# The last nine head pairs of an attention and MLP kernel: q and k loaded by tokens and transposed by DMA

## The chip, the cores and the metric

The kernel runs on one core of one Trainium2 chip. The metric is the device time of one execution in microseconds. A core has TensorE (PE, matrix products into the eight banks of PSUM), ScalarE (ACT), VectorE (DVE), GpSimd (POOL), the queue engine SyncE (SP) and 16 DMA engines. Every engine works through its own list of instructions in order and waits on semaphores. DMAs can be issued from SP, ACT and POOL; a DMA that changes the type from float32 to bfloat16 on the way is issued from POOL in this kernel.

## The reference

```
q, k, v: 8 x 8 heads x 576 tokens x 64, float32
q_d, k_d, v_d = means over groups of 4 tokens           (144 coarse tokens)
out_d     = softmax(q_d k_d^T / 8) v_d, each row repeated 4 times
out_local = softmax over |i - j| < 4 of (q k^T / 8), times v
x   = (out_up + out_local) as 4608 tokens x 512
h   = x @ w_in          (512 x 2048)
out = (h * sigmoid(h)) @ w_out      (2048 x 512), float32
```

The attention is small in arithmetic and rich in instructions; the two products of the MLP are most of the arithmetic.

## The kernel before

The 64 heads are worked in 32 pairs (two heads side by side on 128 partitions). A pair passes through these steps; the letters are the names of the planner's jobs.

- `cq`, `ck`: q and k of the pair are loaded and cast to bfloat16 by one DMA each from POOL (line 676), by rows of 576 numbers: a row holds nine tokens of one head, and the tile qkb has 128 rows (k is loaded with an offset of 64 rows, so a tile holds halves of two pairs). qkb has six buffers.
- `T`: 36 transposes of 64x64 on TensorE (`pe_T`, line 810) turn q and k into [head dimension, token] in two PSUM banks.
- `eq`, `ek`: two copies from PSUM to qT and kT, on ACT from pair 8 on (line 565), which also put the tokens in order.
- `mq`, `mk`: two reductions on DVE (line 845), which sum groups of four tokens.
- `S`: 28 score products on TensorE; then two exps on ACT (line 893) and a product with the band mask on DVE (line 899).
- `Z`: sums of the softmax on TensorE, a small transpose, a reciprocal and a spread on DVE (lines 964, 968, 974).
- `PV`: 28 products with v; then the scaled result xo on DVE (line 990), and the sum of the coarse and the local part into the tile xT on POOL (line 1018).
- v is loaded from SP in two layouts (vs, in runs of 64 numbers, and vq), cast on POOL, and its groups of four are summed on POOL (lines 565, 785, 790).

From pair 8 on the attention's products on TensorE are issued in visits: visit n holds S of pair n, T of pair n+1, PV of pair n−2 and Z of pair n−1. Between the visits TensorE works on the MLP. A G1 block is four products of 512 columns that make one 128-wide slice of h for 512 tokens. ACT takes a tanh of it (line 1043), DVE multiplies (line 1047), which frees the bank, and the result is a slice of gT. A G2 block is four products of 512 columns, a quarter of an output tile of 128 tokens; after four of them ACT copies the tile out (line 1100) and SP stores it. There are 144 blocks of each kind. G1 needs xT of all pairs whose tokens it reads.

The order of all instructions is fixed when the program is built. A planner (`Plan.run`) plays the jobs through with a cost for each, releases buffers and banks, and on each engine starts the ready job with the earliest due time. On TensorE a visit is preferred over MLP blocks from a given number of finished blocks on, and G1 is preferred until it leads G2 by 22 blocks (LEAD). For a DMA a job has a cost (the issue on its engine) and a work (its time on the shared DMA engines), with fixed times before and behind it. Each engine's list is then issued in the order that the plan gave, with the waits that the data need:

```
            op.waits = [...]                      # Prog.op: what the data need
            can = [j for j in ready[e] if self.fits(j)]
            j = pick(now, can) if e == "PE" else min(can, key=lambda j: (j.due, j.idx))
```

So a change of one step can change the order of everything behind it on every engine.

Of the kernel before, what the change touches and what calls it, by code (L numbers as in the profile page):

```python
# [7 lines left out]
ALU = mybir.AluOpType  # L8
# [16 lines left out]
N_QK, N_VS, N_VQ, N_QKB, N_VB, N_VD, N_T, N_P, N_ZR, N_RB, N_XO = 1, 4, 2, 6, 5, 5, 3, 4, 2, 2, 3  # L25
GS_PE = 0
VP_PE = 8

# [466 lines left out]
def bass_hourglass_attn__then__act_silu_kernel(  # L495
# [9 lines left out]
    with kctx:  # L505
# [23 lines left out]

        qk = sb("qk", [128, 2, 576], F32, N_QK)  # L530
        vs = sb("vs", [128, 10, 64], F32, N_VS)
        vq = sb("vq", [128, 4, 256], F32, N_VQ)
# [4 lines left out]
        qT = sb("qT", [128, S_], BF16, N_T)  # L537
        kT = sb("kT", [128, S_ + 16], BF16, N_T)
        qd = sb("qd", [128, SD], BF16, N_T)
# [7 lines left out]
        for name, n, first in (("qk", N_QK, 0), ("vs", N_VS, 0), ("vq", N_VQ, VP_PE), ("vt", 1, VP_PE),  # L547
                               ("qkb", N_QKB, -1), ("vb", N_VB, 0), ("vd", N_VD, 0), ("T", N_T, 0), ("P", N_P, 0),
                               ("zr", N_ZR, 0), ("Rb", N_RB, 0), ("xo", N_XO, 0), ("th", 2, 0), ("osb", 3, 0)):
            L.pool(name, n, first, SW if name == "qk" else ())  # L550

# [61 lines left out]
        def constants():  # L613
# [44 lines left out]
            fill("pads", [(t[:, a:b], 0.0, [], [R(f"{n}{i}")]) for i in range(N_T)  # L658
                          for t, n, a, b in ((kT[i], "kTa", 0, 3), (kT[i], "kTb", 579, 592), (kd[i], "kdp", 144, 192))], -75)
            fill("hot", [(hot[:, i, :], 0.0, [], [R(f"hot{i}")]) for i in range(3)]  # L660
# [19 lines left out]
        def loads(p, order):  # L680
            if p == 0:
                dma("lkx", LD_ENG("kx", 0), lambda: kx[64:128, :], lambda: rows(k, 0, 64, 0), None, lambda: rkx, lambda: "kx",
                    0.45, 0.43, due=order["kx"], take=[("qkb", -1)])
            for x, (t, n, off) in enumerate(((q, 128, 0), (k, 128 if p < NPAIR - 1 else 64, 64))):
# [62 lines left out]
        def casts(p):  # L747
# [28 lines left out]
            def emitv(jb):  # L776
                a, b = S("vs", p), S("vb", p)
                P.op(jb.ran, lambda e: copy(jb.ran, e, vb[b][:, :, :], vs[a][:, :, :]),
                     [R(f"vs{a}{h}{j}") for h in range(2) for j in range(2)] + ([R("vz")] if p == 0 else []), [R(f"vb{b}")])
            J(f"cv{p}", CV_ENG if p < 4 else "POOL", {"POOL": 0.72, "ACT": 0.74}, emitv, pre=[f"lv{p}{h}{j}" for h in range(2) for j in range(2)],  # L780
              port=True, due=D(p, 4.8 if p < 4 else 6.0), take=[("vb", p)], use=[("vs", p)])
# [20 lines left out]
        def pe_T(p):  # L802
            a, b = S("qkb", p), S("qkb", p - 1)
            tiles = ((0, 0, 0, a), (0, 1, 1, a), (1, 1, 0, a), (1, 0, 1, b))
            for r in range(9):
                for j, h, x, n in tiles:
                    t, c = t_home(p, x, r)
                    o = PS[half(h), t, c:c + 32].bitcast(BF16)
                    w = qkb[n][half(j), x, 64 * r:64 * r + 64]
                    P.op("PE", lambda e, o=o, w=w, j=j: e.transpose(o, w, idn[half(j), :]),  # L810
                         [R("idn"), R(f"qkb{n}{x}")], [rB[t]])

        def pe_G(p):
            s, b = S("T", p), bank(("g", p))[0]
            for x, t in enumerate((qT[s][:, :], kT[s][:, 3:579])):
                for r in range(4):
                    mm(PS[:, b, 144 * x:144 * x + 144], idw[:, :], t.rearrange("p (g r) -> p r g", r=4)[:, r, :],
                       [R("idw"), R(f"{'qk'[x]}T{s}")], [rB[b]], r == 0, r == 3)

        def after_T(p):  # L820
# [3 lines left out]
            def evict(x):  # L824
                def emit(jb):
                    s = S("T", p)
                    dst = (qT[s][:, :] if x == 0 else kT[s][:, 3:579]).rearrange("p (g r) -> p g r", r=9)
# [12 lines left out]

            def reduce(x):
                def emit(jb):
                    s = S("T", p)
                    dst, src = (qd[s][:, :], qT[s][:, :]) if x == 0 else (kd[s][:, 0:SD], kT[s][:, 3:579])
                    P.op("DVE", lambda e: e.tensor_reduce(dst, src.rearrange("p (g r) -> p g r", r=4), AX.X, ALU.add),  # L845
                         [R(f"{'qk'[x]}T{s}")], [R(f"{'qk'[x]}d{s}")])
                return emit

            if grp:
                J(f"G{p}", "PE", 1.08, lambda jb: pe_G(p), pre=[f"eq{p}", f"ek{p}", "idw1"], bank=[(("g", p), G_BANKS(p))],  # L850
                  due=D(p, 7.7), use=[("T", p)], kind="A", mm=8)
            for x in range(2):
# [3 lines left out]
                if grp:  # L856
                    J(f"m{n}{p}", G_ENG(p, x), {"ACT": 0.31, "DVE": 0.27}, group(x), pre=[f"G{p}"], bank=[(("g", p), ())],
                      due=D(p, 7.4), use=[("T", p)])
                else:
                    J(f"m{n}{p}", "DVE", 0.74, reduce(x), pre=[f"e{n}{p}"], due=D(p, 7.3), **keys)  # L860

        def pe_S(p):
# [9 lines left out]
            for i in range(5):  # L872
                for h in range(2):
                    for y in range(2):
                        c, n = 58 * i, 58 if i < 4 else 56
                        t = 288 * y + c
                        mm(PS[half(y), bb[h], c:c + n], kT[s][half(h), t:t + 64], qT[s][half(h), t:t + n], rl,
                           [rB[bb[h]]], not bias, True)
# [230 lines left out]
        def tk(p):  # L1109
            return dict(use=[("qkb", p), ("qkb", p - 1)], pre=[f"cq{p}", f"ck{p}", "idn"] + (["ckx"] if p == 0 else [f"ck{p - 1}"])  # L1110
                        , bank=[(("q", p), T_BANKS(p)), (("k", p), T_BANKS(p))])
# [39 lines left out]
        def visit(n):  # L1151
            s, t = n < NPAIR, n + 1 < NPAIR
            z = n - 1 if SPLIT <= n - 1 < NPAIR else None
# [61 lines left out]
        for p in range(SPLIT + 1):  # L1215
            split(p)
        for n in range(SPLIT, NPAIR + LAG):
            visit(n)
# [78 lines left out]
```

## Time and profile before

| | us |
|---|---|
| median of three runs | 340.75 (340.31 to 341.02) |
| the profiled execution, whole | 342.31 |
| its span (first to last instruction) | 340.5 |
| TensorE busy | 326.8 |
| VectorE busy | 229.6 |
| ScalarE busy | 179.0 |
| GpSimd busy | 156.6 |
| one copy to qT or kT on ScalarE, mean | 0.66 |
| one reduction to qd or kd on VectorE, mean | 0.72 |
| issue of one load of q or k on GpSimd | 0.55 |

Busy time says which engine has work, not which one is waited for. TensorE's instructions overlap: one 64x64 transpose is shown with 201 ns, and a whole block of 36 takes about 0.3 us. What a part is worth on TensorE is therefore read from the distance between the starts of what stands before and behind it. "PEld" is the load of the stationary operand, which runs ahead of its product.

### The profile page before, as it was taken

The page shows a single profiled execution, that of the slowest core. Times are in us where ns is not written, and L with a number is a line of the kernel's source. Part 1 is how long each engine was busy: PE and PEld are TensorE (multiplying, and loading weights), DVE is VectorE, ACT ScalarE, POOL GpSimd, SP SyncE. Part 2 cuts the span into 40 slices and gives each one's busy share as a digit, 9 for nine tenths or more (in the row PEclk, how much of TensorE's full clock was granted, in tenths as well). Part 3 has the DMA queues.
Part 4 walks back from the last instruction along what each step waited for, and adds up shares of the span by engine and source line. Part 5 has one row for each costly group of instructions (what it writes and reads, how often), then busy time and mean ns, then how long its engine had stood idle before and what let it go on. Part 6 is the DMA issues. An engine that isn't in the chain of part 4 may idle for free.

```text
span 340.5 us, 10780 instructions
## 1 busy us (share of the span) xinstructions
PE 326.8 (96%) x4623; PEld 213.9 (63%) x4623; DVE 229.6 (67%) x410; ACT 179.0 (53%) x317; POOL 156.6 (46%) x211
## 2 busy tenths in 40 slices
PE   5587999999999999999999999999999999999996
PEld 2465677865555775587557755785577558866544
DVE  6586989866667885788577857796767556754200
ACT  5542756665544765476447645664656416644221
POOL 7363498435679667970698068704400140000000
PEclk9755999999999999999999999999999999999999
DMA  8997879999878976996398339500100010000112
GB/s 168 175 252 156 255 181 212 198 229 234 172 178 195 213 177 151 209 202 174 76 240 180 81 57 249 115 1 33 66 31 2 33 64 31 2 1 31 62 64 92
DMA packets 70666, 44.59 MB, mean 131 GB/s; under 512 B 45914, under 2 KB 63770, under 8 KB 70618
## 3 DMA queue, kind: packets, MB, share of 16 engines
q1 hardware_dynamic: 56378, 28.00, 30.8%
q0 software_dynamic: 13088, 15.36, 26.2%
q8 instruction: 36, 0.59, 0.7%
q10 hardware_dynamic: 1152, 0.54, 0.7%
q14 instruction: 12, 0.10, 0.1%
HBM read 45.61 MB, written 9.44 MB: 162 GB/s over the span
## 4 chain that ended last, share of the span: by engine, by line
PE 92%; DMA 2%; DVE 2%; issue 2%; POOL 1%; ACT 0%; POOLq 0%
PE PS L571 89%; PE PS L810 3%; DMA qkb<-in_k_dram 2%; DVE Pt L899 1%; POOL qkb L676 0%; DVE qd L845 0%; POOL gT L601 0%; DVE Rb L974 0%; DVE qT L565 0%; DVE kd L845 0%; DVE zt L964 0%; DVE zr L968 0%; ACT osb L1076 0%; DVE vd L565 0%; POOL idw L610 0%
## 5 line engine op out<-in xcount | busy, mean ns | idle before, releaser
L571 PE MATMUL PS<-xT,w_in_sb 128*128 128x512 f32 x576 | 141.2, 399 | 0.0
L571 PE MATMUL PS<-w_out_bf,gT 128*128 128x512 bf16 (+1 forms) x592 | 131.3, 374 | 0.0
L571 PEld LDWEIGHTS PS<-xT,w_in_sb 128*128 128x128 f32 x576 | 106.7, 188 | 24.7 <-DVE gT L1047 0.7
L1047 DVE SCALAR_TENSOR_TENSOR gT<-th,PS 128x512 bf16<-128x512 f32 x144 | 96.9, 683 | 37.0 <-ACT th L1043 36.3
L1043 ACT ACTIVATE th<-PS 128x512 f32<-128x512 f32 x144 | 86.1, 599 | 54.2 <-PE PS L571 46.0
L571 PEld LDWEIGHTS PS<-w_out_bf,gT 128*128 128x128 bf16 x592 | 54.7, 98 | 62.9 <-issue 3.5
L1018 POOL TENSOR_TENSOR xT<-xo 128x576 fp32r<-128x576 f32 (+5 forms) x48 | 43.5, 919 | 51.5 <-DVE xo L990 51.4
L565 POOL CAST vb<-vs 128x640 bf16<-128x640 f32 x32 | 24.4, 767 | 57.3 <-PE PS L571 42.5
L1100 ACT ACTIVATE osb<-PS 128x512 f32<-128x512 f32 x35 | 21.1, 603 | 53.6 <-PE PS L571 53.6
L893 ACT ACTIVATE Pt<-PS 128x576 bf16<-128x576 f32 x32 | 20.8, 649 | 33.0 <-PE PS L571 32.8
L785 POOL TENSOR_TENSOR vt<-vq 128x512 f32<-128x512 f32 x24 | 30.8, 1285 | 10.0 <-DMA vq<-in_v_dram 9.9
L990 DVE TENSOR_TENSOR xo<-PS,Rb 128x720 f32<-128x720 f32 x32 | 28.6, 893 | 5.1 <-PE PS L571 4.9
L974 DVE STREAM_TRANSPOSE Rb<-zr 128x768 f32<-128x768 f32 x32 | 30.9, 964 | 0.1
L899 DVE TENSOR_TENSOR Pt<-Pt,mask 128x576 bf16<-128x576 bf16 x24 | 16.3, 677 | 20.9 <-ACT Pt L893 20.9
L565 ACT ACTIVATE qT<-PS 128x576 bf16<-128x576 bf16 x30 | 19.8, 659 | 9.4 <-PE PS L810 9.4
L810 PE MATMUL PS<-idn,qkb 64*64 64x64 bf16 x1152 | 17.5, 201 | 7.5 <-issue 3.9
L845 DVE TENSOR_REDUCE qd<-qT 128x144 bf16<-128x576 bf16 x32 | 22.9, 716 | 1.5 <-ACT qT L565 1.4
L845 DVE TENSOR_REDUCE kd<-kT 128x144 bf16<-128x576 bf16 x32 | 23.0, 718 | 0.0
L964 DVE STREAM_TRANSPOSE zt<-PS 128x96 f32<-128x96 f32 x32 | 8.8, 274 | 20.2 <-PE PS L571 20.2
L565 ACT ACTIVATE kT<-PS 128x576 bf16<-128x576 bf16 x30 | 20.0, 665 | 1.6 <-PE PS L810 1.6
L810 PEld LDWEIGHTS PS<-idn,qkb 64*64 64x64 bf16 x1152 | 14.2, 115 | 9.5 <-issue 4.5
L676 POOL DMA_DIRECT2D qkb<-in_k_dram x31 | 17.1, 553 | 5.1 <-PE PS L810 5.1
(56 smaller groups left out, 229.3 us busy)
## 6 DMA issues: line engine op xcount, KB each, us to landing
vs<-in_v_dram SPq DMA_DIRECT2D x123, 80.0 KB, 4.6
out_dram<-osb SPq DMA_DIRECT2D x35, 256.0 KB, 3.6
vq<-in_v_dram SPq DMA_DIRECT2D x24, 256.0 KB, 4.3
qkb<-in_q_dram POOLq DMA_DIRECT2D x31, 144.0 KB, 5.0
qkb<-in_k_dram POOLq DMA_DIRECT2D x30, 144.0 KB, 5.4
w_in_sb<-in_moe_w_in_dram POOLq DMA_DIRECT2D x4, 1024.0 KB, 7.4
w_out_bf<-in_moe_w_out_dram POOLq DMA_DIRECT2D x4, 512.0 KB, 14.3
vq<-in_v_dram SPq DMA_DIRECT2D x48, 32.0 KB, 3.9
```

What stands on the lines that cost most here:

```text
L565: return e.activation(out_, in_, AF.Copy) if eng == "ACT" else e.tensor_copy(out_, in_)
L571: P.op("PE", lambda t: t.matmul(out_, lhsT, rhs, start=start, stop=stop, skip_group_check=True), r, w)
L785: P.op("POOL", lambda g: g.tensor_tensor(vt[:, :, :], vq[n][:, :, 0:128], vq[n][:, :, 128:256], ALU.add), [R(f"vqm{n}"), R(f"vqe{n}0"), R( ...
L810: P.op("PE", lambda e, o=o, w=w, j=j: e.transpose(o, w, idn[half(j), :]), [R("idn"), R(f"qkb{n}{x}")], [rB[t]])
L845: P.op("DVE", lambda e: e.tensor_reduce(dst, src.rearrange("p (g r) -> p g r", r=4), AX.X, ALU.add), [R(f"{'qk'[x]}T{s}")], [R(f"{'qk'[x]} ...
L893: P.op("ACT", lambda e: e.activation(d[:, :, :], PS[:, b[0]:b[1] + 1, a:e_], AF.Exp, scale=sc), [rB[b[0]], rB[b[1]]], [R(f"P{m}" if local ...
L974: P.op("DVE", lambda e: e.transpose(Rb[n][:, :].rearrange("p (c q) -> p c q", q=32), zr[z][:, :].unsqueeze(2).to_broadcast([128, 24, 32])) ...
L990: P.op("DVE", lambda e: e.tensor_tensor(xo[x][:, :, :], PS[:, bb[0]:bb[1] + 1, 0:360], Rb[u][:, :].rearrange("p (x c) -> p x c", x=2)[:, : ...
L1018: P.op("POOL", lambda g, dst=dst, in0=in0, in1=in1: g.tensor_tensor(dst, in0, in1, ALU.add), [R(f"xo{x}")], xblk(kc, t + a, t + e_))
L1043: P.op("ACT", lambda e: e.activation(th[x][:, :], PS[:, b, :], AF.Tanh, scale=0.5), [rB[b]], [R(f"th{x}")])
L1047: P.op("DVE", lambda e: e.scalar_tensor_tensor(gT[j % 2][:, f, :], th[x][:, :], 1.0, PS[:, b, :], ALU.add, ALU.mult), [rB[b], R(f"th{x}")] ...
L1100: P.op("ACT", lambda e, s=S("osb", n), b=bank(key)[0]: e.activation(osb[s][:, :], PS[:, b, :], AF.Copy, scale=0.5), [rB[bank(key)[0]]], [R ...
```

## The change

From pair 23 to pair 31 (`DTS`), q and k no longer go through qkb, TensorE and PSUM. Each of them is loaded by two DMAs from POOL (one for each head) into one of four tiles tq: 96 partitions, six blocks, and in each block the 64 numbers of a token of both heads. A run of 64 numbers is 256 bytes in DRAM and 128 bytes as bfloat16. Then one DMA issued from ACT transposes the six blocks of 96x128 into qT or kT. The reductions, the scores and all behind them are as before. kT's data begin at column 16 instead of 3. Three of the four tq tiles lie in the memory of qk, which only pair 0 uses. A load of pair p+2 waits until the transpose of pair p has read the tile. The casts of v may go to ACT or POOL for these pairs; in the order that the planner makes, they stay on POOL.

On TensorE nine blocks of 36 transposes fall away; on ACT 18 copies are replaced by 18 issues of a transpose; on POOL 18 loads are replaced by 36 smaller-grained ones. The due times, costs and thresholds of all other jobs are unchanged. The planner makes a new order from pair 22's visit on.

```
+DTS = tuple(range(23, NPAIR))
+KB = 16
+C_WORK, X_WORK, X_COST = 1.35, 0.95, 1.22
+X_ENG = "ACT"
...
+        tq3 = qk[0][:, :, :].rearrange("p a b -> p (a b)").bitcast(BF16)
+        tq1 = sb("tq", [128, 768], BF16)
+        tq = [tq3[:, 768 * i:768 * i + 768] for i in range(3)] + [tq1[:, :]]
...
+                if p in DTS:
+                    def emitc(jb, x=x, t=t):
+                        u = S("tq", 2 * DTS.index(p) + x)
+                        d = tq[u][0:96, :].rearrange("p (a h d) -> p a h d", a=6, h=2)
+                        for h in range(2):
+                            P.op("POOL", lambda e, h=h: e.dma_start(d[:, :, h, :], bass.AP(
+                                tensor=t.tensor, offset=t.offset + (2 * p + h) * S_ * D_, ap=[[64, 96], [96 * 64, 6], [1, 64]])),
+                                [], [R(f"tq{u}")], f"tq{u}", after=gates(["cq0", "ck0"] + list(order.get(("gate", p), ()))))
+                    J(f"c{'qk'[x]}{p}", "POOL", 1.46, emitc, work=C_WORK, gran=0.018, take=[("tq", 2 * DTS.index(p) + x)], due=D(p, 26.0),
+                      pre=["cq0", "ck0", f"c{chr(113 - 6 * x)}{p - 1}!"] + list(order.get(("gate", p), ())))
+                    continue
...
-            J(f"cv{p}", CV_ENG if p < 4 else "POOL", {"POOL": 0.72, "ACT": 0.74}, emitv, pre=[f"lv{p}{h}{j}" for h in range(2) for j in range(2)],
+            J(f"cv{p}", CV_ENG if p < 4 else "POOL" if p not in DTS else ("POOL", "ACT"), {"POOL": 0.72, "ACT": 0.74}, emitv, pre=[f"lv{p}{h}{j}" for h in range(2) for j in range(2)],
...
+        def transpose_dma(p):
+            for x in range(2):
+                def emit(jb, x=x):
+                    s, u = S("T", p), S("tq", 2 * DTS.index(p) + x)
+                    o = qT[s][:, :] if x == 0 else kT[s][:, KB:KB + S_]
+                    P.op(jb.ran, lambda e: e.dma_start_transpose(
+                        o.rearrange("p (a b) -> p a b", a=6), tq[u][0:96, :].rearrange("p (a c) -> p a c", a=6)),
+                        [R(f"tq{u}")], [R(f"{'qk'[x]}T{s}")], f"{'qk'[x]}T{s}")
+                n = "qk"[x]
+                J(f"e{n}{p}", X_ENG, X_COST, emit, work=X_WORK, gran=0.018, pre=[f"c{n}{p}"], use=[("tq", 2 * DTS.index(p) + x)], take=[("T", p)], due=D(p, 9.0))
+            reduces(p)
...
-            s, t = n < NPAIR, n + 1 < NPAIR
+            s, t = n < NPAIR, n + 1 < NPAIR and n + 1 not in DTS
...
+        for p in DTS:
+            transpose_dma(p)
```

More of the change, by code (lines that the diff above doesn't have):

```diff
@@ L537, in bass_hourglass_attn__then__act_silu_kernel @@
         qT = sb("qT", [128, S_], BF16, N_T)
-        kT = sb("kT", [128, S_ + 16], BF16, N_T)
+        kT = sb("kT", [128, S_ + 32], BF16, N_T)
         qd = sb("qd", [128, SD], BF16, N_T)
@@ L548, in bass_hourglass_attn__then__act_silu_kernel @@
                                ("qkb", N_QKB, -1), ("vb", N_VB, 0), ("vd", N_VD, 0), ("T", N_T, 0), ("P", N_P, 0),
-                               ("zr", N_ZR, 0), ("Rb", N_RB, 0), ("xo", N_XO, 0), ("th", 2, 0), ("osb", 3, 0)):
-            L.pool(name, n, first, SW if name == "qk" else ())
+                               ("zr", N_ZR, 0), ("Rb", N_RB, 0), ("xo", N_XO, 0), ("th", 2, 0), ("osb", 3, 0), ("tq", 4, 0)):
+            L.pool(name, n, first, SW if name == "qk" else DTS if name == "qkb" else ())
         PS = E(nc.psum_tensor("PS", [128, 8, 512], F32))
@@ L658, in constants @@
             fill("pads", [(t[:, a:b], 0.0, [], [R(f"{n}{i}")]) for i in range(N_T)
-                          for t, n, a, b in ((kT[i], "kTa", 0, 3), (kT[i], "kTb", 579, 592), (kd[i], "kdp", 144, 192))], -75)
+                          for t, n, a, b in ((kT[i], "kTa", KB - 3, KB), (kT[i], "kTb", KB + S_, KB + S_ + 13), (kd[i], "kdp", 144, 192))], -75)
             fill("hot", [(hot[:, i, :], 0.0, [], [R(f"hot{i}")]) for i in range(3)]
@@ L683, in loads, with emitk @@
                     0.45, 0.43, due=order["kx"], take=[("qkb", -1)])
-            for x, (t, n, off) in enumerate(((q, 128, 0), (k, 128 if p < NPAIR - 1 else 64, 64))):
+            for x, (t, n, off) in enumerate(((q, 128, 0), (k, 128 if p < NPAIR - 1 and p + 1 not in DTS else 64, 64))):
+                if p in DTS:
[9 more added lines that the diff above has]
+                    continue
+                if x and p - 1 in DTS:
+                    def emitk(jb):
+                        u = S("qkb", p)
+                        for j in range(2):
+                            P.op("POOL", lambda e, j=j: e.dma_start(qkb[u][half(j), 1, :], rows(k, p, 64, 64 - 64 * j)), [], [R(f"qkb{u}1")],
+                                 f"qkb{u}1", after=gates(order.get(("gate", p), ())))
+                    J(f"ck{p}", "POOL", 1.1, emitk, work=0.87, gran=0.106, take=[("qkb", p)], due=D(p, 26.0), pre=list(order.get(("gate", p), ())))
+                    continue
                 if p in SW:
@@ L802, in pe_T @@
         def pe_T(p):
-            a, b = S("qkb", p), S("qkb", p - 1)
+            a = S("qkb", p)
+            b = a if p - 1 in DTS else S("qkb", p - 1)
             tiles = ((0, 0, 0, a), (0, 1, 1, a), (1, 1, 0, a), (1, 0, 1, b))
@@ L814, in pe_G @@
             s, b = S("T", p), bank(("g", p))[0]
-            for x, t in enumerate((qT[s][:, :], kT[s][:, 3:579])):
+            for x, t in enumerate((qT[s][:, :], kT[s][:, KB:KB + S_])):
                 for r in range(4):
@@ L818, in pe_G, with reduces, reduce, emit @@
                        [R("idw"), R(f"{'qk'[x]}T{s}")], [rB[b]], r == 0, r == 3)
+        def reduces(p):
+            def reduce(x):
+                def emit(jb):
+                    s = S("T", p)
+                    dst, src = (qd[s][:, :], qT[s][:, :]) if x == 0 else (kd[s][:, 0:SD], kT[s][:, KB:KB + S_])
+                    P.op("DVE", lambda e: e.tensor_reduce(dst, src.rearrange("p (g r) -> p g r", r=4), AX.X, ALU.add),
+                         [R(f"{'qk'[x]}T{s}")], [R(f"{'qk'[x]}d{s}")])
+                return emit
+            for x in range(2):
+                n = "qk"[x]
+                J(f"m{n}{p}", "DVE", 0.74, reduce(x), pre=[f"e{n}{p}"], due=D(p, 7.3), take=[("T", p)])
+        def transpose_dma(p):
+            for x in range(2):
+                def emit(jb, x=x):
[4 more added lines that the diff above has]
+                        [R(f"tq{u}")], [R(f"{'qk'[x]}T{s}")], f"{'qk'[x]}T{s}")
+                n = "qk"[x]
+                J(f"e{n}{p}", X_ENG, X_COST, emit, work=X_WORK, gran=0.018, pre=[f"c{n}{p}"], use=[("tq", 2 * DTS.index(p) + x)], take=[("T", p)], due=D(p, 9.0))
+            reduces(p)
         def after_T(p):
@@ L826, in emit @@
                     s = S("T", p)
-                    dst = (qT[s][:, :] if x == 0 else kT[s][:, 3:579]).rearrange("p (g r) -> p g r", r=9)
+                    dst = (qT[s][:, :] if x == 0 else kT[s][:, KB:KB + S_]).rearrange("p (g r) -> p g r", r=9)
                     b = bank(("qk"[x], p))[0]
@@ L839, in group @@
                 return emit
[L841 to L847, printed above, removed]
             if grp:
@@ L858, in after_T @@
                       due=D(p, 7.4), use=[("T", p)])
-                else:
-                    J(f"m{n}{p}", "DVE", 0.74, reduce(x), pre=[f"e{n}{p}"], due=D(p, 7.3), **keys)
+            if not grp:
+                reduces(p)
         def pe_S(p):
@@ L876, in pe_S @@
                         t = 288 * y + c
-                        mm(PS[half(y), bb[h], c:c + n], kT[s][half(h), t:t + 64], qT[s][half(h), t:t + n], rl,
+                        mm(PS[half(y), bb[h], c:c + n], kT[s][half(h), KB - 3 + t:KB + 61 + t], qT[s][half(h), t:t + n], rl,
                            [rB[bb[h]]], not bias, True)
@@ L1109, in tk @@
         def tk(p):
-            return dict(use=[("qkb", p), ("qkb", p - 1)], pre=[f"cq{p}", f"ck{p}", "idn"] + (["ckx"] if p == 0 else [f"ck{p - 1}"])
+            return dict(use=[("qkb", p)] + [("qkb", p - 1)] * (p - 1 not in DTS), pre=[f"cq{p}", f"ck{p}", "idn"] + (["ckx"] if p == 0 else [f"ck{p - 1}"] * (p - 1 not in DTS))
                         , bank=[(("q", p), T_BANKS(p)), (("k", p), T_BANKS(p))])
```

## The prediction

> **What bounds the kernel now.** I read the page's busy shares first, then the slices, then the chain of waits, then the groups, and last the timeline around two visits. The page:
>
> ```profile
> span 340.5 us, 10780 instructions
> PE 326.8 (96%) x4623; PEld 213.9 (63%) x4623; DVE 229.6 (67%) x410; ACT 179.0 (53%) x317; POOL 156.6 (46%) x211
> ...
> PEclk9755999999999999999999999999999999999999
> DMA  8997879999878976996398339500100010000112
> ...
> PE 92%; DMA 2%; DVE 2%; issue 2%; POOL 1%; ACT 0%; POOLq 0%
> ...
> L1043 ACT ACTIVATE th<-PS 128x512 f32<-128x512 f32 x144 | 86.1, 599 | 54.2 <-PE PS L571 46.0
> ...
> L565 ACT ACTIVATE qT<-PS 128x576 bf16<-128x576 bf16 x30 | 19.8, 659 | 9.4 <-PE PS L810 9.4
> L810 PE MATMUL PS<-idn,qkb 64*64 64x64 bf16 x1152 | 17.5, 201 | 7.5 <-issue 3.9
> ...
> L676 POOL DMA_DIRECT2D qkb<-in_k_dram x31 | 17.1, 553 | 5.1 <-PE PS L810 5.1
> ```
>
> TensorE is the bound: 92% of the chain, clock full from the fifth slice on, no idle slice after the first four. Whatever leaves its stream inside the visits shortens the kernel, if nothing new makes it wait. The DMA digits are high up to about slice 25 and near zero behind it: the transfer engines have room in the second half of the stretch that the change touches. The timeline of TensorE's weight loads gives a visit with a transpose block (pair 30's, the first three lines) and one without (pair 31's):
>
> ```profile
> 264.58 0.24 PEld L571 LDWEIGHTS PS<-qT,kT 64*64 64x64 bf16 x20 [0.42 <-issue]
> 264.82 0.44 PEld L810 LDWEIGHTS PS<-idn,qkb 64*64 64x64 bf16 x36
> 265.93 4.00 PEld L571 LDWEIGHTS PS<-w_out_bf,gT 128*128 128x128 bf16 x20
> ...
> 270.35 0.24 PEld L571 LDWEIGHTS PS<-qT,kT 64*64 64x64 bf16 x20 [0.42 <-issue]
> 271.35 0.55 PEld L571 LDWEIGHTS PS<-w_out_bf,gT 128*128 128x128 bf16 x4
> ```
>
> From the first load of the scores to the first of the next expert block it is 265.93 − 264.58 = 1.35 us with the block and 271.35 − 270.35 = 1.00 us without.
>
> **The change part by part.**
>
> TensorE's transposes. Nine blocks of 36 go (pairs 23 to 31). The chain of waits in order of time lists the last nine pieces of line 810 with 0.31, 0.35, 0.31, 0.31, 0.31, 0.34, 0.31, 0.31 and 0.35 us: 2.9 us. The two visits above would say 9 x 0.35 = 3.15. I take −2.9; it lies wholly on the path.
>
> TensorE's order. The planner writes another order, and the built program shows it: the visits of pairs 23 to 31 come earlier among the expert blocks (the scores of pair 31 follow 192 blocks instead of 215), and G1 and G2 blocks alternate more: 40 changes from G1 to G2 instead of 18. In the alternating tail of the old run a pair takes 1.803 us (first loads of G2 at 302.40, 304.20, 306.00); G1 in a row takes 0.905 (tanh starts 296.26, 297.16, 298.07), G2 in a row 0.86 (104 loads in 18.93 us, 32 of them halves: 88 wholes of 0.215, four to a block). So a change costs 0.04 us, 22 more cost 0.8; four more visits follow a G1, which I put at 0.2 in all. Sum +1.0, ends 0.5 and 1.5.
>
> ScalarE. It loses 18 copies of 0.66 us and gets 18 issues of a DMA transpose, in order between the tanh instructions that free G1's banks. No row shows such an issue. Below stands the cheapest issue on SP, 0.39 us (vq, line 721); above, 2.3 us, if each of its six blocks of 96 tokens costs one such issue. Nearest is the issue of v (five blocks of 64 rows), 0.60 to 0.64 us; six blocks with a rearrangement are more than that, and the planner's own entry is 1.22, in a table whose other entries agree with rows (tanh 0.61 against 0.599, copy 0.66 against 0.659, v issue 0.64). I take 1.2. Where does that fit? The densest stage is from pair 27's exps to pair 28's: ten tanh at 0.55 (two back to back take 1.09 at 223.62), 0.94 for the two exps (216.49 to 217.43), four issues: 6.4 + 4 x 1.2 = 11.2 us, against nine G1 blocks and a visit on TensorE, 9 x 0.905 + 1.0 = 9.15. It overflows by 2.1. G1 has four banks, and a block's natural way through tanh and multiply is 1.8 us, so 4 x 0.905 − 0.905 − 1.8 = 0.9 us is forgiven: about 1.2 us of stall, of which I take 0.7, because the blocks of transposes no longer hold two of those banks. The next dense stage (pairs 22 to 23) is 6.4 + 3 x 1.2 = 10.0 against 10.05 and fits. Ends: 0 at 0.39 us and about 10 us at 2.3.
>
> GpSimd. Each pair's two loads (0.55 us each) become four of 576 runs. The rows: 0.55 us for 128 runs, 0.78 us for 512 (w_in, line 740). On that slope 0.82: 36 x 0.82 − 18 x 0.55 = +19.6 us. Between the scores of pair 22 and the last PV TensorE has, in the new order, 45 G1 blocks of 0.905, 25 G2 of 0.86 and eleven visits of about 1.0, together 73 us or 7.3 for each of ten pairs; GpSimd holds some 57 us of work there. From pair 25 on each load also waits for the landing of the transpose two pairs earlier, and the v sums, casts and the adds into xT queue behind it. That waiting is covered as long as G1 blocks ready in xT stand ahead: in the new order TensorE has six blocks (5 us) between the last PV and the second G1 block that needs the last pairs, where 3 us suffice (0.9 for xo, 1.5 for the adds, releases). Cost 0; without cover it is the third rival.
>
> The loads themselves. 1152 packets for q, as many for k, 256 bytes read and 128 written, 72 per transfer engine each. Rows: 25 ns a packet where v's 256-byte packets dominate (30 to 60 us: 3927 packets in 20.8% of 16 engines) and 110 ns for today's row-wise cast packets of 2304 bytes (205 to 216 us: 591 packets in 36.9%). I take 25, the same size: 1.8 us each and 3.6 a pair, of 7.3 us that a pair has. The other end, 15.8 a pair, would make the transfer engines the bound by 8.5 us a pair. Cost 0 here, as transposes are issued about 11 us or more ahead of their scores in the new order.
>
> [...]
>
> VectorE keeps its work: two reductions a pair, now released by a DMA. It grows dense: measured start to start, 46 multiplies of 0.61 and some 3.8 us for each of ten visits make about 67 us in those 73. In the old run it was busy 13.5 of 16.0 us (216.3 to 232.3) and TensorE waited for it 0.3 us. I count 0 here and keep it in the range.
>
> Sum: −2.9 + 1.0 + 0.7 = −1.2 us. The profiled execution took 342.31 us (span 340.5 and 1.8 around it), 1.56 above the median 340.75. So 341.1 for a profiled execution, and 339.5 against the median.
>
> **Rivals.**
>
> One, slower: ScalarE's queue. If the issue costs 1.6 us, the stage of pairs 27 to 28 overflows by 12.8 − 9.15 = 3.7, that of 22 to 23 by 1.1; less 0.9 it is 4 us of stall, +1.0 − 2.9 + 4.0 = +2.1: 342.9. It decides from about 1.35 us on. For it: no row has such an issue, and tanh cannot be delayed long. Against it: ScalarE is idle for half of these slices, and only one stage is tight.
>
> Two, slower: token loads land late. ScalarE then stands at a transpose with tanh behind it. For the q and k of pairs 25 and 26 I count 0 to 1 us between landing and issue in the new order, so a load 2 us longer (50 ns a packet, where also a pair's 7.2 us fill its 7.3) costs 2 us at once and as much again at later pairs: −1.9 + 4 to 5, 343.5. For it: cast packets at 110 ns. Against it: packets of this size at 25 ns, and idle transfer engines behind 220 us.
>
> Three, slower by a little: GpSimd and VectorE hinder each other. The mask multiply (line 899) takes 393 ns at best, 458 in the middle and 1590 at worst, and GpSimd will be busier beside it. 0.5 us more on each of nine in a stretch that is 92% full: +3 us after slack, 341.8.
>
> Four, even: the gain is eaten, 340.75.
>
> That the change does not do what it says is excluded by the built order: nine blocks are gone and 18 transposes stand on ScalarE.
>
> **How the numbers follow.** Forecast case (338.0 to 340.0) 0.48; even, within 0.2% (0.68 us, about what this measurement can tell), 0.10; ScalarE 0.20; loads 0.13; GpSimd and VectorE 0.09. Faster 0.48, same 0.10, slower 0.42. Time 339.5. The range starts at 338.0 (3.15 saved, 0.5 given back, no stall) and goes to 344.5, which takes in the three rivals at their prices and leaves out their worst ends, about 2 in 10 with what lies below.
>
> **What would show it.** Right: the last nine pieces of line 810 gone, visits of 1.00 us from pair 22 on, no new releaser of TensorE over 1 us between 181 and 255 us, and ScalarE's wait for the token loads near zero. Wrong: TensorE idle on tanh or multiply inside the G1 runs before pairs 23 and 28 (first rival), ScalarE waiting for a DMA into tq (second), mask multiplies beyond 0.6 us in the middle (third). An issue over 1.35 us, or packets over 50 ns, would make the forecast wrong.

## The result: slower by 0.7%

The changed kernel takes 343.55 us (median of seven executions, 341.69 to 345.32), the kernel before, timed beside it, 341.02 (339.86 to 341.76). The ratio is 1.0072, 95% interval 1.0051 to 1.0093. I had forecast 339.5, faster; the time is inside the range I gave, on the other side of no change. The profiled execution is the longest of the seven: 345.32 us, span 343.5. The granted clock was not lower in it (0.975, and 0.970 in the profile of before), so the clock does not explain the loss.

The page of the changed kernel, in the order in which I read the one of before (code lines moved: 571 is now 578, 810 is 837, 893 is 936, 899 is 942, 1043 is 1086, 1047 is 1090; the token loads are line 697, the transposes 864):

```profile
span 343.5 us, 10125 instructions
PE 326.5 (95%) x4299; PEld 208.3 (61%) x4299; DVE 232.2 (68%) x410; ACT 168.5 (49%) x299; POOL 171.8 (50%) x229
...
PEclk9965899999999999999999999999999999999999
DMA  8997879999888977999299999994000010000112
...
q0 software_dynamic: 31808, 15.37, 33.3%
...
q10 hardware_dynamic: 12096, 3.20, 6.6%
...
PE 78%; DMA 9%; DVE 5%; POOL 3%; issue 3%; ACT 0%; POOLq 0%
...
L942 DVE TENSOR_TENSOR Pt<-Pt,mask 128x576 bf16<-128x576 bf16 x24 | 21.3, 889 | 12.4 <-ACT Pt L936 10.9
L852 DVE TENSOR_REDUCE qd<-qT 128x144 bf16<-128x576 bf16 x32 | 23.1, 720 | 1.6 <-DMA qT<-qk 1.1
L837 PE MATMUL PS<-idn,qkb 64*64 64x64 bf16 x828 | 12.4, 199 | 7.4 <-issue 4.9
```

TensorE's work is gone as planned (828 transposes instead of 1152), but it is 78% of the chain instead of 92%. The DMA digits, before at 5 in slice 26 and at 0 to 2 behind it, stay at 9 through slice 27. And the mask multiply, of which there are still 24, takes 889 ns in the mean instead of 677. TensorE's weight loads at the visit of pair 26:

```profile
211.09 0.24 PEld L578 LDWEIGHTS PS<-qT,kT 64*64 64x64 bf16 x20 [0.42 <-issue]
...
212.09 0.55 PEld L578 LDWEIGHTS PS<-w_out_bf,gT 128*128 128x128 bf16 x4
```

A visit without a block takes 1.00 us, as I had read. Where the time went is seen from the first score loads of the visits, which cut both runs into stretches:

| stretch | before | after | difference |
|---|---|---|---|
| start to visit 11 | 92.07 | 92.70 | +0.6 |
| visit 11 to 22 | 88.97 | 90.40 | +1.4 |
| of it visit 18 to 19 | 16.89 | 18.73 | +1.8 |
| visit 22 to the end | 159.4 | 160.4 | +1.0 |

The first row is start-up, which differs by a microsecond between two profiles of one program: visit 11 comes at 91.88 us in a_yield and at 92.97 in its repetition a_yield_b. The second was no part of my sum: up to visit 22 TensorE does the same work in the same order in both. The timeline of VectorE and that of GpSimd (vt and vd are the two steps that sum v in groups of four, vb is a cast of v) show what happened between visits 18 and 19:

```profile
148.51 3.17 DVE L942 TENSOR_TENSOR Pt<-Pt,mask 128x576 bf16<-128x576 bf16 x1
151.60 1.27 DVE L1090 SCALAR_TENSOR_TENSOR gT<-th,PS 128x512 bf16<-128x512 f32 x2
```

```profile
147.52 0.74 POOL L572 CAST vb<-vs 128x640 bf16<-128x640 f32 x1
148.20 1.30 POOL L811 TENSOR_TENSOR vt<-vq 128x512 f32<-128x512 f32 x1
149.45 1.22 POOL L1061 TENSOR_TENSOR xT<-xo 128x576 fp32r<-128x576 f32 x1
150.62 0.73 POOL L816 TENSOR_TENSOR vd<-vt 128x256 bf16<-128x256 f32 x1
151.30 1.47 POOL L697 DMA_DIRECT2D qk<-in_q_dram  x2
```

The multiply starts under vt and ends at 151.68, only after xT and vd have also gone through and GpSimd has turned to issuing a load. In the kernel before, the same multiply started 0.02 us ahead of another neighbour, vd, and took about an eighth of that; there it was vd that took longer, 0.99 us instead of the 0.73 that it takes after:

```profile
148.16 0.42 DVE L899 TENSOR_TENSOR Pt<-Pt,mask 128x576 bf16<-128x576 bf16 x1
...
148.18 0.99 POOL L790 TENSOR_TENSOR vd<-vt 128x256 bf16<-128x256 f32 x1
```

In the changed kernel the multiplies that free G1's banks stand behind it in VectorE's list, and TensorE waits for them, 1.45 and 0.32 us:

```profile
152.33 1.69 PEld L578 LDWEIGHTS PS<-xT,w_in_sb 128*128 128x128 f32 x8 [1.45 <-DVE gT L1090]
...
154.34 1.70 PEld L578 LDWEIGHTS PS<-xT,w_in_sb 128*128 128x128 f32 x8 [0.32 <-DVE gT L1090]
```

That is nearly all of the 1.8 us. It falls before the first pair that the change touches because GpSimd's new order begins at 144.57 us, and not at pair 22's visit as TensorE's does: there the token loads of pair 23 stand, four issues that take 3.0 us, where the kernel before has two loads of 1.1 us at 144.21. Behind them vt comes after the cast instead of ahead of it, and xT ahead of vd. Behind visit 22 two stretches stand out, as the experiments will show: visit 23 to 24 (7.71 us) and visit 27 to 28 (11.45 us).

### The profile page after: what moved, and what is told of

It reads as the page before. It is cut to its first block, busy times and chain, and to the rows that moved or that the text cites. A ratio compares the mean times of both kernels' runs of the same rounds, so it can differ in the third digit from the quotient of the medians.

```text
span 343.5 us, 10125 instructions
## 1 busy us (share of the span) xinstructions
PE 326.5 (95%) x4299; PEld 208.3 (61%) x4299; DVE 232.2 (68%) x410; ACT 168.5 (49%) x299; POOL 171.8 (50%) x229
## 3 DMA queue, kind: packets, MB, share of 16 engines
q0 software_dynamic: 31808, 15.37, 33.3%
## 4 chain that ended last, share of the span: by engine, by line
PE 78%; DMA 9%; DVE 5%; POOL 3%; issue 3%; ACT 0%; POOLq 0%
PE PS L578 76%; DMA qT<-qk 2%; DMA qkb<-in_k_dram 2%; PE PS L837 2%; DVE Pt L942 2%; DMA kT<-qk 2%; DMA qk<-in_q_dram 2%; DMA qk<-in_k_dram 1%; DVE gT L1090 1%; POOL qk L697 1%; POOL qkb L683 1%; DVE xo L1033 1%; DVE qd L852 0%; POOL xT L1061 0%; POOL vt L811 0%
## 5 line engine op out<-in xcount | busy, mean ns | idle before, releaser
L578 PE MATMUL PS<-xT,w_in_sb 128*128 128x512 f32 x576 | 152.4, 409 | 2.2 <-DVE gT L1090 2.1
L578 PE MATMUL PS<-w_out_bf,gT 128*128 128x512 bf16 (+1 forms) x592 | 134.4, 374 | 0.7 <-DVE gT L1090 0.7
L1090 DVE SCALAR_TENSOR_TENSOR gT<-th,PS 128x512 bf16<-128x512 f32 x144 | 95.9, 679 | 50.2 <-ACT th L1086 47.3
L578 PEld LDWEIGHTS PS<-w_out_bf,gT 128*128 128x128 bf16 x592 | 53.2, 98 | 65.6 <-issue 9.7
L942 DVE TENSOR_TENSOR Pt<-Pt,mask 128x576 bf16<-128x576 bf16 x24 | 21.3, 889 | 12.4 <-ACT Pt L936 10.9
L837 PE MATMUL PS<-idn,qkb 64*64 64x64 bf16 x828 | 12.4, 199 | 7.4 <-issue 4.9
L816 POOL TENSOR_TENSOR vd<-vt 128x256 bf16<-128x256 f32 x24 | 18.3, 764 | 0.5
L572 ACT ACTIVATE qT<-PS 128x576 bf16<-128x576 bf16 x21 | 13.8, 658 | 8.5 <-PE PS L837 8.5
L936 ACT ACTIVATE Pd<-PS 128x432 bf16<-128x432 f32 x32 | 17.0, 532 | 0.0
L578 PEld LDWEIGHTS PS<-qT,kT 64*64 64x64 bf16 x640 | 9.0, 111 | 12.0 <-issue 11.0
```

The costliest lines, as they stand in the source:

```text
L572: return e.activation(out_, in_, AF.Copy) if eng == "ACT" else e.tensor_copy(out_, in_)
L578: P.op("PE", lambda t: t.matmul(out_, lhsT, rhs, start=start, stop=stop, skip_group_check=True), r, w)
L936: P.op("ACT", lambda e: e.activation(d[:, :, :], PS[:, b[0]:b[1] + 1, a:e_], AF.Exp, scale=sc), [rB[b[0]], rB[b[1]]], [R(f"P{m}" if local ...
L942: P.op(jb.ran, lambda e: e.tensor_tensor(Pt[m][:, :, :], Pt[m][:, :, :], mask[:, :].unsqueeze(1).to_broadcast([128, 2, 288]), ALU.mult), [ ...
L1090: P.op("DVE", lambda e: e.scalar_tensor_tensor(gT[j % 2][:, f, :], th[x][:, :], 1.0, PS[:, b, :], ALU.add, ALU.mult), [rB[b], R(f"th{x}")] ...
```

## The experiments

Theory A: GpSimd's new list holds more instructions back to back, the mask multiply is kept waiting by them, and TensorE waits for what is queued behind it. Theory B: transposes and token loads land late, and the queue of ScalarE and VectorE behind them delays TensorE. All ratios are to the kernel before, timed beside each kernel, with 95% intervals; medians are of 6 to 12 executions (7 for the changed kernel).

| kernel | median, us | ratio | visit 18 to 19 | visit 22 to end |
|---|---|---|---|---|
| before | 341.02 to 341.73 | 1 | 16.89 | 159.4 |
| after | 343.55 | 1.0072 (1.0051 to 1.0093) | 18.73 | 160.4 |
| b_red | 340.17 | 0.9970 (0.9949 to 0.9992) | 16.93 | 158.9 |
| a_red | 339.57 | 0.9940 (0.9918 to 0.9962) | 16.92 | 157.3 |
| b_yield | 341.23 | 0.9988 (0.9962 to 1.0013) | 17.00 | 159.1 |
| a_yield | 340.52 | 0.9972 (0.9943 to 1.0001) | 17.07 | 157.9 |
| a_y18 | 340.99 | 0.9983 (0.9965 to 1.0002) | 16.96 | 159.0 |
| a_sixth | 341.71 | 1.0006 (0.9989 to 1.0023) | 18.74 | 158.0 |
| a_sixth_red | 338.85 | 0.9913 (0.9888 to 0.9938) | 16.92 | 157.2 |
| a_light_red | 339.73 | 0.9934 (0.9909 to 0.9960) | 16.92 | 157.2 |
| after2 | 343.11 | 1.0035 (1.0007 to 1.0063) | 18.68 | 159.4 |
| a_red_T | 342.93 | 1.0039 (1.0011 to 1.0067) | 16.90 | 160.6 |
| a_y25 | 343.58 | 1.0051 (1.0023 to 1.0078) | 17.16 | 160.7 |
| a_ysixth | 339.21 | 0.9910 (0.9878 to 0.9942) | 17.04 | 157.7 |
| a_w | 342.48 | 1.0009 (0.9980 to 1.0037) | 18.71 | 157.8 |
| a_yw | 339.25 | 0.9907 (0.9875 to 0.9939) | 17.05 | 157.8 |
| a_yw2 | 344.98 | 1.0074 (1.0045 to 1.0103) | 17.06 | 164.3 |
| a_yield_b | 339.99 | 0.9953 (0.9930 to 0.9977) | 17.09 | 157.7 |
| a_yw_b | 340.27 | 0.9946 (0.9924 to 0.9968) | 17.06 | 157.8 |

The medians carry what start-up and the spread of executions do; the last two columns, from one profile each, are free of the start.

**A one-input step in the multiply's place (b_red, a_red).** In both kernels the mask multiply becomes a reduction of half of Pt, which has one input and about the same length; the mask is not applied, and what reads Pt no longer waits for VectorE's step either.

```
-                    Pt[m][:, :, :], Pt[m][:, :, :], mask[...]..., ALU.mult), ...
+                P.op(jb.ran, lambda e: e.tensor_reduce(scr[:, :], Pt[m][:, 0, :].rearrange("p (g r) -> p g r", r=4), AX.X, ALU.add), ...
```

> The kernel before, but the mask multiply on VectorE (pairs 8 to 31) is replaced by a reduction of half of Pt into a scratch tile: about as long (0.4 us), one input instead of two; the mask is not applied, so the far scores stay in the softmax. Theory A (VectorE's mask multiply is kept waiting by GpSimd's work, and that is where the change lost its time): the multiplies of before lost only about 4 us of VectorE time, nearly all of it covered, so within 0.5 us of before. Theory B (the transposes land late and hold VectorE and GpSimd): the same, 341.0 +- 0.5.

> The changed kernel with the same replacement. Theory A: the seven microseconds by which the multiplies were stretched beyond 0.42 us vanish, and with them some 4 us of TensorE's waiting: 339 to 340.3, under before. Theory B: at most 0.5 us better than the changed kernel, 343.

The reduction takes 0.39 to 0.46 us wherever it falls, in both kernels. The changed kernel falls by 4 us to 339.57 and the kernel before by 1.3, to 340.17, more than the 0.5 that I expected: it too had multiplies that were held. So without these held multiplies the change is worth −1.6 us in the trace (157.3 against 158.9 from visit 22 on), and −0.6 by the medians, whose intervals overlap. Visit 18 to 19 is 16.92 again, 23 to 24 6.60 instead of 7.71, 27 to 28 9.49 instead of 11.45. My sum for the same thing was −1.2, or −1.9 without ScalarE's 0.7.

**The same with everything computed (b_yield, a_yield).** After each mask multiply in the plan's order, GpSimd's next computing instruction waits for it.

```
+            if jb.ran == "POOL" and jb.port and pend:
+                P.extra = pend[:]
...
+            if jb.name[0] == "k" and jb.name[1:].isdigit():
+                pend.append(P.streams[jb.ran][-1])
```

> The kernel before; after each mask multiply in the plan's order, GpSimd's next computing instruction waits for that multiply. Both theories: within 0.7 us of before, 340.3 to 341.7; GpSimd is not on the path there.

> The changed kernel with the same waits on GpSimd; everything is computed. Theory A: a multiply is then held by at most one GpSimd instruction (1.3 us), the 2 to 3 us cases go, and half of the loss comes back: 340.5 to 342. Theory B: no gain, 343 to 344.5, as GpSimd's loads come later.

The multiply can still be held by one instruction (1.52 us at 148.22, and 0.8 to 1.4 at four other places), no longer by two or three. That gives 3 us back in the changed kernel, and next to nothing in the one before. The order of GpSimd's instructions is as it was, everything is computed, and the added waits alone take the loss away (the median is 0.3% below the kernel before, with an interval that reaches 1.0001); that settles theory A for most of the loss.

**One wait (a_y18).** The same, for pair 18 alone.

> The changed kernel, with one wait added: GpSimd's next computing instruction waits for the mask multiply of pair 18 (in the changed kernel's trace it starts at 148.51 and takes 3.17 us). Nothing is left out. Theory A (that multiply is kept waiting by three GpSimd instructions in a row, and TensorE loses 1.8 us by it, before the first changed visit): the multiply takes at most 1.5 us, the visits of pairs 18 and 19 lie 16.9 to 17.3 us apart instead of 18.73, and the whole falls by 1.0 to 2.0 us, to 341.5 to 342.5, with the multiplies behind 190 us as long as before, or about so. Theory B (the loss lies behind pair 22, in late transposes and ScalarE's queue): those two visits may come closer, but the whole stays within 0.5 us of 343.5, since TensorE waits for the transposes afterwards.

```profile
147.91 1.29 DVE L946 TENSOR_TENSOR Pt<-Pt,mask 128x576 bf16<-128x576 bf16 x1
```

```profile
147.58 1.30 POOL L815 TENSOR_TENSOR vt<-vq 128x512 f32<-128x512 f32 x1
149.28 1.23 POOL L1065 TENSOR_TENSOR xT<-xo 128x576 fp32r<-128x576 f32 x1 [0.41 <-DVE Pt L946]
```

The multiply ends at 149.20, 0.32 us after vt; xT waited 0.41 us for it, and visit 19 comes 16.96 us after visit 18. The whole fell by 2.6 us against the first timing, more than I expected of A: the multiplies behind pair 22 fell differently too (2.32 us at pair 23, but 0.97 instead of 1.76 at pair 27, and no wait for a transpose). One moved wait changes which instructions meet later on.

**Lighter transposes (a_sixth, a_sixth_red), lighter loads as well (a_light_red).**

```
-                        o.rearrange("p (a b) -> p a b", a=6), tq[u][0:96, :].rearrange("p (a c) -> p a c", a=6)),
+                        o[:, 0:96], tq[u][0:96, 0:128]),
```

> The changed kernel, but each transpose by DMA handles only the first of its six blocks of 96 tokens (five sixths of q and k of the last nine pairs are left out; all else as it was). Theory A: the issue on ScalarE gets shorter and the landing too, but GpSimd and VectorE work as before, so the mask multiply at about 148 us still takes about 3 us, those behind 190 us still up to 1.5 us or more, and the time falls by no more than 1 us: 342.5 to 344. Theory B: TensorE waits for late transposes or for tanh behind their issues, so the time falls by 2 to 4 us, to 339.5 to 341.5.

> As before with one block of six transposed, and in place of the mask multiply the one-input reduction on VectorE (mask left out). Against the changed kernel with that reduction alone (339.57 us, 66.2 us from the visit of pair 22 to that of 31, 9.49 between those of 27 and 28) it shows what issue and landing of the transposes cost once VectorE is free. My prediction's +0.7 us for the stall between the visits of 27 and 28 would go: 338.6 to 339.3, 65.2 to 65.9 us, 9.1 to 9.2. If the transposes cost nothing: 339.3 to 339.9 and the same distances. If late landings cost more than I saw (rival): below 338.5.

> As the last one, and the loads by tokens bring only the first of six blocks too (five sixths of q and k of the last nine pairs are not loaded; mask left out). It leaves TensorE's new order almost alone. If the loads' packets (about 32 ns each) cost nothing, as I predicted, it stays within 0.5 us of the last one; if they slow other DMAs or GpSimd's queue, it falls by 1 us or more, below 338. By my sum (nine blocks of transposes less, the new order for +1.0, nothing else) it ends 1.9 us below the kernel before with the same reduction (340.17): 338.3.

With the reduction the transposes' weight matters little: visit 27 to 28 is 9.40 instead of 9.49, visit 22 to the end 157.2 instead of 157.3, and with light loads the same 157.2. So landing and packets together cost 0.1 us where VectorE is not held. The issue is not priced by this: with one block it still takes ScalarE 1.11 us (in the middle, a_ysixth) instead of 1.21. The lower median of the second kernel (338.85) is where my +0.7 would have put it, but it has no counterpart in these stretches. With the multiply kept (a_sixth) the result lies between the two expectations: visit 18 to 19 is 18.74 as theory A said, but behind visit 22 it gains 2.4 us on the changed kernel's first profile. There is no late transpose in it, and the multiplies of pairs 23 and 27 take 0.57 and 0.41 us; those of pairs 26 and 28 take 2.06 and 2.11 and cost at most 0.7 us, by which visit 27 to 28 (10.15) stays above 9.49. I had held these collisions for fixed; they are not.

**The changed kernel again (after2).**

> The changed kernel once more, word for word, for a second profile. Its executions so far lie between 341.69 and 345.32 us and the profiled one was the longest, so part of what its trace shows may be that one execution. By theory A the multiply of pair 18 is again about 3.2 us long and the visits of pairs 18 and 19 lie 18.7 us apart (the kernel with one block of six transposed showed the same 3.16 us), since what comes before it is the same each time; behind pair 22 the multiplies fall otherwise, and the way from the visit of pair 22 to that of 31, 69.2 us in the first profile, lies between 66.8 and 69.2. Whole: 342.5 to 344.5. By theory B (late transposes) VectorE waits for a transpose again at the visit of pair 27, and that way is again about 69 us.

Median 343.11, executions from 341.24 to 346.31 us. From visit 22 on it takes 159.4 us, no more than the kernel before. The multiply of pair 18 takes 3.15 us and costs 1.8 us in this profile too. Between visits 27 and 28 there were 11.45 us in the first profile and 10.41 here; the multiply of pair 27 is the same (1.76 us), but VectorE waits for a transpose only 0.19 us. In the first:

```profile
218.03 0.75 DVE L852 TENSOR_REDUCE qd<-qT 128x144 bf16<-128x576 bf16 x1 [1.12 <-DMA qT<-qk]
...
221.50 1.76 DVE L942 TENSOR_TENSOR Pt<-Pt,mask 128x576 bf16<-128x576 bf16 x1
```

So of the 2.0 us above 9.49, about 1 belongs to the late transpose and 1 to the multiply: theory B has a share, in some executions.

**The blocks put back (a_red_T).** a_red with 36 transposes of the identity ahead of the scores in each of the last nine visits.

```
+            if p in DTS:
+                for r in range(9):
+                    for j, h, x in ((0, 0, 0), (1, 0, 1), (1, 1, 1), (0, 1, 0)):
+                        P.op("PE", lambda e, ...: e.transpose(o, idn[half(j), :], idn[half(j), :]), ...)
```

> The changed kernel with the one-input reduction in place of the mask multiply (mask left out), and 36 transposes of 64x64 (of the identity, into the scores' banks ahead of the scores) put back on TensorE in each visit of the last nine pairs: the new order with the old amount of work. Against the same kernel without them (339.57 us, span 339.2, 157.35 us from the visit of pair 22 to the end) it prices the nine blocks, and against the kernel before with the reduction (340.17, 158.9 us on the same way) the new order. My terms: blocks +2.9 and order +1.0, so 160.0 to 160.4 us on that way and 342.2 to 342.8 whole. Rival: the new order costs nothing and the blocks only what the two kernels differ by, 1.6 us: 158.9 us, 341.2.

From visit 22 on it takes 160.6 us, 3.3 more than a_red: nine blocks at 0.37. Against b_red's 158.9, with the same work on TensorE in the old order, the new order and all else that the change brings cost 1.7 us (by the medians, from two timings, 2.8). I had 1.0 for the order and 0.7 for ScalarE; this run does not part the two.

**From pair 25 on (a_y25).** `DTS = tuple(range(25, NPAIR))`, with the waits.

> The changed kernel from pair 25 on only (seven pairs instead of nine), with GpSimd's next computing instruction waiting for each mask multiply; everything is computed. Seven blocks save 2.25 us by my price, and the planner's order has 29 changes from G1 to G2 instead of 40, so 0.45 us less for the order; GpSimd and the DMAs carry 8 token loads less. Theory A: 340.0 to 340.8, no worse than with nine pairs (340.52), and below 341.23, the kernel before with the same waits. Theory B: the fewer transposes fall together with other DMAs, the better, so below 340. If changes of the order cost nothing, it is 0.6 us slower than with nine pairs: 341.1.

A miss: 343.58, though no multiply takes over 0.46 us between 128 and 215 us. Behind that three are held in spite of the waits (1.05, 1.24 and 2.16 us at pairs 26 to 28), and TensorE waits only 0.2 us behind them. The loss is elsewhere: VectorE stands at a transposed tile with G1's multiplies behind it, and TensorE waits longer than that, in VectorE's and TensorE's timelines:

```profile
218.74 0.75 DVE L856 TENSOR_REDUCE qd<-qT 128x144 bf16<-128x576 bf16 x1 [1.92 <-DMA qT<-qk]
```

```profile
220.14 1.69 PEld L582 LDWEIGHTS PS<-xT,w_in_sb 128*128 128x128 f32 x8 [2.46 <-DVE gT L1094]
```

The reduction waited 1.92 us, up to 218.74, for its transpose to land. A smaller dose of the change is not a smaller effect: the planner makes another order, and this one has a late landing in it.

**Is the late landing a cause of its own? (a_ysixth, a_w, a_yw, a_yw2).** a_ysixth is a_yield with light transposes. a_w changes two numbers of the planner to the trace's (and with them the order), a_yw adds the waits, and a_yw2 tells 2.5 us for a transpose.

```
-C_WORK, X_WORK, X_COST = 1.35, 0.95, 1.22
+C_WORK, X_WORK, X_COST = 2.3, 1.26, 1.22
```

> The changed kernel with GpSimd waiting once for each mask multiply, and each transpose by DMA moving only the first of its six blocks (five sixths of q and k of the last nine pairs are left out). Nothing but the transposes' landing and their issue differs from the kernel with the waits (340.52 us, 66.74 us from the visit of pair 22 to that of 31). If late transposes are a cause of their own: 339.0 to 339.9, and 66.0 to 66.3 us on that way. If they only follow from held multiplies: within 0.4 us of 340.5, 66.5 to 66.9 us.

> The changed kernel with one difference: the planner is told the transfer time of a token load and of a transpose as the trace has them (1152 packets of 32 ns over 16 DMA engines, 2.3 us; 672 of 30 ns, 1.26 us) instead of 1.35 and 0.95. Everything is computed, no wait is added. Its order has 26 changes from G1 to G2 instead of 40 and spreads the last visits further. If late transposes and the dense order cost what I read (about 1 us for the transposes, 0.6 for the changes): 341.3 to 342.5, no wait of VectorE for a transpose, the multiply of pair 18 as it falls. If only the multiplies count: 343 to 344, like the changed kernel.

> The last kernel with GpSimd waiting once for each mask multiply. Both causes taken away, everything computed: 339.0 to 340.0, below the kernel with the waits alone (340.52) and below the kernel before by 0.4 to 0.7%. If the planner's numbers do nothing: 340.5.

> As the last one, with 2.5 us told for a transpose: an order with 20 changes from G1 to G2, nearly as few as in the kernel before (18). By my price of 0.04 us a change it gains 0.2 us on the last one: 338.8 to 339.9. If the price of the order lies elsewhere (visits after a G1 block, the tail), there is no difference; if the later visits leave too few pairs ready in front of G1, TensorE waits for xT and it is slower than the last one by 0.5 us or more.

a_w keeps the 3.17 us multiply of pair 18 (visit 18 to 19: 18.71), but from visit 22 on it needs 157.8 us without any added wait, 1.7 and 2.6 less than the two profiles of the changed kernel: VectorE waits for no transpose, and behind pair 23 (1.55) no multiply exceeds 0.44 us. a_yw has both, 339.25. a_ysixth came as low, 339.21, which spoke for a cause of its own; its profile did not (66.49 us from visit 22 to 31, against 66.74 in a_yield). Side by side:

> The changed kernel with GpSimd waiting once for each mask multiply, once more, beside the next one on the same chip. If late transposes are a cause of their own that only some executions show, its times spread over 3 us or more, the median lies 0.7 to 1.5 us above the next kernel's, and its profile may show VectorE waiting for a transpose. If the lower time of the kernels with a lighter or better known transfer came from the chip or from chance, the two lie within 0.5 us.

> The same waits, and the planner told the transfer times of the trace (2.3 and 1.26 us), once more. 339.0 to 340.0 us, below the kernel before by 0.5 to 1.1%, times within 2 us of each other, and no wait of VectorE for a transpose above 0.5 us.

a_yield_b took 339.99 us and a_yw_b 340.27 (0.3 above the range that I gave it). They lie 0.3 us apart, and a_yield_b needs the same 66.48 us from visit 22 to 31 as a_ysixth: with the multiplies protected, the landing costs nothing that these runs can tell. I put the gap between the first timings down to chance. Both beat the kernel before, by 0.5%, and the changed one. The page of a_yw_b and its group of multiplies:

```profile
span 338.6 us, 10134 instructions
PE 324.0 (96%) x4299; PEld 209.2 (62%) x4299; DVE 224.0 (66%) x410; ACT 169.2 (50%) x300; POOL 168.3 (50%) x228
...
L946 DVE TENSOR_TENSOR Pt<-Pt,mask 128x576 bf16<-128x576 bf16 x24 | 12.4, 518 | 13.8 <-ACT Pt L940 13.8
```

518 ns a multiply instead of 889, and the span 4.9 us shorter than in the first profile of the changed kernel. a_yw2 went the other way, as its last alternative said: with the later visits, GpSimd's adds into xT come too late for G1, and its weight loads and products wait for them (the two rows overlap), most of the 6 us that it loses to a_yw:

```profile
PEld PS L582 <- POOL xT L1065: 4.8, 2, 2.5
PE PS L582 <- POOL xT L1065: 3.9, 2, 2.1
```

## Why the prediction was wrong

- **The step that failed is "VectorE keeps its work … I count 0 here", and with it the price of the third rival.** I put 0.5 us on each of nine mask multiplies "in a stretch that is 92% full", from a row with 458 ns in the middle and 1590 at worst, and gave it 0.09. The multiplies were held by up to 2.75 us (3.17 less 0.42), one of them in front of the stretch that I looked at. In the profiled execution this cost 1.8 us at pair 18, 1.1 at pair 23 and 1 at pair 27: 3.9 of TensorE's time (2.21 us at pair 28 cost nothing). My 1590 ns is the longest from 90 us on; over the whole span the row of before says 2542, and the timeline shows what lay under that multiply, a cast and vt:

```profile
L899 DVE TENSOR_TENSOR Pt<-Pt,mask x24: 393/458/2542, 76.1 to 272.7; 128x576 bf16<-128x576 bf16 x24
...
81.37 2.54 DVE L899 TENSOR_TENSOR Pt<-Pt,mask 128x576 bf16<-128x576 bf16 x1
...
81.63 0.73 POOL L565 CAST vb<-vs 128x640 bf16<-128x640 f32 x1
82.31 1.27 POOL L785 TENSOR_TENSOR vt<-vq 128x512 f32<-128x512 f32 x1
83.66 0.84 POOL L790 TENSOR_TENSOR vd<-vt 128x256 bf16<-128x256 f32 x1
```

It cost TensorE too: visit 10 to 11 took 6.53 us, and 5.75 with the reduction in the multiply's place (b_red). So the trace of before showed both the mechanism and its price, and the built order of GpSimd around each multiply was the thing to compare.
- **TensorE's blocks, −2.9**: right, 3.3 measured (a_red_T).
- **TensorE's order, +1.0, and ScalarE's stall, +0.7**: together 1.7 in the trace, as in my sum, but the split was probably off. The issue is 1.21 us, as I took it from the planner's entry, but in a_red visit 27 to 28 takes 9.49 us where I had reckoned 9.15 without any stall, and TensorE waits there for a bank of G1 only once, 0.22 us. So at most 0.3 us of the 0.7 is seen at the place where I put it, and the agreement of the sum is in part luck. The first rival is out:

```profile
L864 ACTq DMA_TRANSPOSE qT<-qk x9: 1212/1214/1366, 177.2 to 232.6; - x9
```

```profile
221.84 1.23 PEld L579 LDWEIGHTS PS<-xT,w_in_sb 128*128 128x128 f32 x6 [0.22 <-DVE gT L1090]
```

- **GpSimd, 0**: no wait of TensorE for xT appears in the changed kernel, and an issue takes 0.74 us (I had 0.82). But the longer issues moved everything behind them in GpSimd's list, from 144.57 us on, and I gave that no price.
- **The loads, 0 for 25 ns a packet and for transposes "issued about 11 us or more ahead of their scores"**: 32 ns a packet, an estimate from the two pages: 36 x 576 token packets replace 18 x 128 row-wise ones at 110 ns, and queue q0 went from 26.2% of 16 engines to 33.3%. A transpose landed 2.5 to 8.2 us after its issue, with the DMA engines at 9 of 10 in slices 21 to 27; no row of before has such a landing, so its 0 in my sum was not shown. That made some transposes late, 1.1 us in the first profile and 0.2 in the second. The second rival had ScalarE wait for loads; what cost time was VectorE waiting for a transpose. Late landings were not the main cause, but they had a share, and in a_y25 they were enough.
- **The sum.** From visit 22 on: −1.6 for TensorE (a_red against b_red), +3.1 for held multiplies and the late transpose (160.4 against 157.3), −0.5 because the kernel before had held multiplies too (159.4 against 158.9): +1.0. With +1.4 ahead of it and +0.6 of start-up that is the 3.0 us between the two spans.
- **What I named as a sign**, "mask multiplies beyond 0.6 us in the middle (third)", was the right sign in the wrong statistic: the middle is 458 ns, as before; the mean (889) and the longest (3171) show it.

## What to carry to other kernels

When a change moves instructions on GpSimd, go one by one through those VectorE instructions whose row has a worst case far above the middle (here the mask multiply of before, 458 ns in the middle and 2542 at worst) and look which GpSimd instructions the new order puts beside each, also ahead of the place that was changed; a mean or a median hides three bad meetings out of 24. If VectorE's instruction has others behind it that free TensorE's banks, let GpSimd's next computing instruction wait for it: here GpSimd stood for 20 us in all by it (a_yield), off the path, and 2.6 to 3.0 us of the whole came back. And tell a planner the transfer times that the trace shows, but read its new order before believing it: a step further (a_yw2) lost nearly 6 us.

## What the runs showed of the hardware

- The mask multiply on VectorE, which has two inputs and took 0.39 to 0.46 us where it was not held, was passed over by several GpSimd instructions that stand back to back: 3.17, 3.15, 3.16 and 3.17 us at pair 18 in four profiles (after, after2, a_sixth, a_w), and at most 1.53 there where the next instruction had to wait. In the first of them vt, xT and vd passed ahead of it. A one-input reduction in the same place never took over 0.46.
- It is not always passed over. In the kernel before, the multiply of pair 20 was held by a cast, then went ahead of vd, which stood right behind the cast, and vd took 0.94 us instead of 0.73. What decides it, no run here shows:

```profile
169.56 1.01 DVE L899 TENSOR_TENSOR Pt<-Pt,mask 128x576 bf16<-128x576 bf16 x1 [1.99 <-ACT Pt L893]
...
169.55 0.72 POOL L565 CAST vb<-vs 128x640 bf16<-128x640 f32 x1 [0.53 <-PE PS L571]
170.22 0.94 POOL L790 TENSOR_TENSOR vd<-vt 128x256 bf16<-128x256 f32 x1
```

- At pair 18 it was held longer by three GpSimd instructions than by one: in a_y18, beside vt alone, it took 1.29 us and ended 0.32 us after vt; in after, beside vt, xT and vd, it took 3.17 us and ended 0.33 us after vd (151.68 against 151.35).
- Whether GpSimd lets the multiply through while it issues a DMA is open. In after the multiply at 106.26 took its 0.46 us beside an issue that lasted to 106.60, and at pair 18 the loads begin at 151.30 and the multiply ends at 151.68; but in after2 the multiply of pair 23 stood from 196.02 beside an issue that lasted to 196.44, as long as it takes by itself, and ended only at 198.01, after the xT that followed (196.45 to 197.67).
- A DMA transpose costs ScalarE nearly the same for one block as for six: 1.11 us in the middle (a_ysixth) against 1.21 (after). I had argued in part from the number of blocks; the right price came from the planner's entry, not from that reason.
- The same program meets these collisions differently from execution to execution: the multiply of pair 23 took 1.45 us in after and 1.99 in after2, and VectorE waited 1.12 and 0.19 us for the same transpose. The spread of the times does not measure this: 12 executions of after2 lie 5.1 us apart, but 12 of a_red_T, with no multiply to hold, lie 4.3 apart.
